# Four kilobytes of unused space behind each eight rows of an input in DRAM

## The chip, the core and the metric

The kernel runs on one core of a Trainium2 chip. The metric is the device time of one execution in microseconds (us). A core has engines that run side by side: TensorE (PE, with its weight loads shown apart as PEld), VectorE (DVE), ScalarE (ACT), GpSimd (POOL), and SyncE (SP), which here only issues DMAs. Sixteen DMA engines move data between DRAM and the on-chip memory SBUF, which has 128 partitions. Matmuls write to PSUM; DVE or ACT copy it from there to SBUF, which is called an eviction here.

## The reference

`x` is a 2048 x 1024 matrix in bf16. Two spectral filters A and B act on the same `x`, and a gate, one number for each row, mixes their results:

```python
g = sigmoid((x * gate_w).sum(-1, keepdims=True))
X = rfft2(x);  a = irfft2(X * (A_w_r + 1j*A_w_i));  b = irfft2(X * (B_w_r + 1j*B_w_i))
return g * a + (1 - g) * b
```

The inputs `A_x`, of which the kernel reads only one copy, and the four weight arrays of 2048 x 513 are read from DRAM, and a 2048 x 1024 result in bf16 is written.

## The kernel before

The Fourier transforms are written as small matmuls with constant matrices. The host sorts the rows of `x` so that a pair of row tiles (`j` and `j+1`) makes one block of 128 partitions by 2 by 1024 elements: `x_in` has the shape (8, 128, 2, 1024), so a partition's row of a block is 4096 bytes and a block is 512 KB without gaps. The columns are sorted so that sums and differences fold them.

L208 loads the eight blocks into the tiles `XR[0]` to `XR[7]` (`xr` in the profile). Blocks 0 and 7 are loaded in two halves of 256 KB, the others in one DMA, so there are ten DMAs, all issued by SP and all ahead of the constants and weights (L238 to L255), which SP issues in the same order behind them. SP waits before an issue until an earlier DMA has landed whose counter it reuses, eight DMAs back. ACT issues three small loads at the start, `f1` (L198), `gws` (L200, 16 bytes for each partition) and `sg` (L202, 4 bytes for each partition).

An order written out by hand (ORDER, a string of steps) sets what each engine does. Its first lines are the forward transform along the rows: `Vj` (function `xfold`, L295 and L296) forms a sum and a difference of `x[j]` on DVE, `rj` and `fj` (function `f1`, L312 and L321) are the matmuls with `x[j]`, or with what `xfold` made of it, as weights, and their evictions to `y` (L278 on ACT, L280 on DVE). For tiles 10 to 15 the steps `E` and `O` do the same for two tiles at once (L324). Then, for each of eight units `n` and both parities of the column frequency, `F` (f2, L375) transforms along the columns, `G` (f3, L394) goes on along the rows, `c` (L415) multiplies with the weights on DVE, and `i` (L453) begins the inverse. `F0` reads a part of `y` from every tile, so it waits for all of `x`.

The inverse stores its rows to scratch in DRAM (L461, `sc<-rl`) and fetches them back in another order (L470, `xr<-sc` and `ro<-sc`). A fetch reads 64 rows of 4096 bytes, each 32 KB behind the one before it. After that come `j` (L483, with the gate), `k` and `D` (L498 to L532), and the sums that make the output (L551 to L582).

Of the kernel before, what the change touches and what calls it, by code (L numbers as in the profile page):

```python
# [12 lines left out]
D = 1024  # L13
# [144 lines left out]
def gated_mix(ctx, tc, x_in, we_in, wo_in, gw_in, out):  # L158
    nc = tc.nc
# [44 lines left out]
    XR = [big.tile([P, 2064], BF16, name=f"xr{v}") for v in range(8)]  # L204
    RO = [big.tile([P, 2064], BF16, name=f"ro{v}") for v in range(8)]
    x = [XR[j // 2][:, 1024 * (j % 2):1024 * (j % 2) + 1024] for j in range(16)]
    for j0, n in ((0, 1), (1, 1)) + tuple((j, 2) for j in range(2, 14, 2)) + ((14, 1), (15, 1)):
        nc.sync.dma_start(XR[j0 // 2][:, 1024 * (j0 % 2):1024 * (j0 % 2 + n)].rearrange("p (j d) -> p j d", j=n), x_in[j0 // 2, :, j0 % 2:j0 % 2 + n, :])  # L208
    FD = const.tile([P, 2, 2, 2, 256], BF16, name="fd")
    IG = const.tile([P, 2, 4, 256], BF16, name="ig")  # L210
    WF = const.tile([P, NT, 3, 64], BF16, name="wf")
# [446 lines left out]
```

## Time and profile before

| | us |
|---|---|
| median of 3 runs | 114.53 |
| lowest and highest run | 112.67, 117.09 |
| the profiled execution | 113.11 |
| its span, first to last instruction | 111.3 |

The granted TensorE clock was 1.0 of full speed in the span. The DMA queues moved 37.07 MB in 18594 packets. The profile gives the busy time of each engine, groups of instructions by line of the code, who waited for whom, and when each DMA was issued and landed; times inside it count from the start of the span. "x<-y" is a tile written from a tile read, with buffer numbers left out. A few lines of the page on DMA, with the number of issues, the size of each and the median time from issue to landing:

```
xr<-sc SPq DMA_DIRECT2D x16, 256.0 KB, 5.2
ro<-in_we_dram SPq DMA_DIRECT2D x7, 516.0 KB, 8.4
xr<-in_x_dram SPq DMA_DIRECT2D x6, 512.0 KB, 8.4
xr<-in_x_dram SPq DMA_DIRECT2D x4, 256.0 KB, 5.7
```

### The profile page before, as it was taken

The numbers are of one execution on the slowest core, as the hardware profiler recorded it, in microseconds if no ns is written. First come the engines' busy times: TensorE is split into PE (matmuls) and PEld (weight loads), VectorE is DVE, ScalarE is ACT, GpSimd is POOL, SyncE is SP. The second block draws the span as 40 slices with busy tenths as digits, with TensorE's granted clock in tenths as the row PEclk, the third lists the DMA queues.
The fourth block names the chain that finished last, engine by engine and source line by source line (L and its number), as shares of the span: only waits on it lengthen the run. The fifth ranks groups of instructions, "written<-read, shape, count | busy, mean of one in ns | idle before, by whom it ended". The sixth has DMA issues, their size and how long they took to land. (4 is left out here: it accounts for less than half of the span.)

```text
span 111.3 us, 4030 instructions
## 1 busy us (share of the span) xinstructions
PE 99.1 (89%) x1656; PEld 68.5 (62%) x1656; DVE 92.3 (83%) x145; ACT 94.0 (84%) x185; POOL 7.4 (7%) x14
## 2 busy tenths in 40 slices
PE   5959989799999999999999999995999775999740
PEld 2339979475556658656765677654699564664430
DVE  0169957399899999999999999995989869699770
ACT  2246977599899999999999999999799798999740
POOL 1000000121592000000000000000000000000000
PEclk9999999999999999999999999999999999999999
DMA  3899999999999998995999999999995789998974
GB/s 106 223 361 415 405 397 406 414 411 388 412 397 409 398 333 262 367 392 181 260 359 334 363 316 386 362 317 378 322 276 217 224 228 358 399 408 358 366 281 128
DMA packets 18594, 37.07 MB, mean 333 GB/s; under 512 B 2188, under 2 KB 11024, under 8 KB 18576
## 3 DMA queue, kind: packets, MB, share of 16 engines
q1 hardware_dynamic: 17696, 36.37, 90.5%
q10 hardware_dynamic: 848, 0.45, 1.4%
q8 instruction: 13, 0.21, 0.7%
q14 instruction: 5, 0.04, 0.1%
q0 software_dynamic: 32, 0.00, 0.0%
HBM read 24.23 MB, written 12.58 MB: 331 GB/s over the span
## 5 line engine op out<-in xcount | busy, mean ns | idle before, releaser
L453 PE MATMUL pt<-p,wi 64*64 64x512 bf16 x488 | 30.6, 377 | 0.0
L278 ACT CAST rl<-pt 128x512 bf16<-128x512 f32 x47 | 28.6, 920 | 0.7 <-PE pt L453 0.7
L415 DVE TENSOR_TENSOR p<-X,ro 128x4096 bf16<-128x4096 bf16 x11 | 25.1, 2293 | 0.4 <-ACT V L344 0.3
L278 ACT CAST T<-pt 128x512 bf16<-128x512 f32 (+1 forms) x40 | 23.2, 721 | 1.6 <-PE pt L532 0.6
L453 PEld LDWEIGHTS <-wi 64*64 64x64 bf16 x488 | 16.1, 106 | 9.6 <-issue 1.5
L278 ACT CAST X<-pt 128x512 bf16<-128x512 f32 x27 | 17.5, 824 | 0.9 <-PE pt L394 0.9
L278 ACT CAST V<-pt 128x512 bf16<-128x512 f32 x28 | 16.3, 690 | 1.6 <-PE pt L483 1.5
L278 ACT CAST y<-pt 128x512 bf16<-128x512 f32 x21 | 11.2, 627 | 5.6 <-PE pt L321 4.1
L375 PE MATMUL pt<-fd,y 128*128 128x256 bf16 x128 | 15.9, 273 | 0.0
L375 PEld LDWEIGHTS <-y 128*128 128x128 bf16 x128 | 11.6, 98 | 4.3 <-issue 2.9
L280 DVE CAST rl<-pt 128x512 bf16<-128x512 f32 x17 | 11.2, 677 | 0.1
L394 PE MATMUL pt<-T,wf 64*64 64x512 bf16 (+2 forms) x192 | 10.5, 307 | 0.6 <-issue 0.6
L498 PE MATMUL pt<-ig,V 128*128 128x256 bf16 x88 | 10.8, 273 | 0.0
L574 DVE TENSOR_TENSOR rl<-wo,T 128x1024 bf16<-128x1024 bf16 (+1 forms) x18 | 9.2, 569 | 1.6 <-ACT T L278 1.2
L498 PEld LDWEIGHTS <-V 128*128 128x128 bf16 x88 | 8.2, 98 | 1.5 <-issue 0.4
L415 DVE TENSOR_TENSOR p<-X,wo 128x4096 bf16<-128x4096 bf16 x4 | 9.1, 2274 | 0.0
L280 DVE CAST y<-pt 128x512 bf16<-128x512 f32 x11 | 7.4, 686 | 2.1 <-PE pt L324 2.0
L278 ACT CAST p<-pt 128x512 bf16<-128x512 f32 x15 | 8.5, 604 | 0.3 <-PE pt L498 0.2
L394 PEld LDWEIGHTS <-wf 64*64 64x64 bf16 x192 | 5.6, 107 | 3.3 <-issue 1.2
L369 POOL TENSOR_SCALAR ro<-ro 128x8 bf16<-128x8 bf16 x7 | 5.8, 850 | 22.6 <-DMA ro<-in_we_dram 22.6
L483 PE MATMUL pt<-eab,ro 128*128 128x64 bf16 x128 | 5.0, 193 | 2.6 <-DMA ro<-sc 1.9
L483 PEld LDWEIGHTS <-ro 128*128 128x128 bf16 x128 | 4.5, 98 | 3.8 <-issue 2.5
(57 smaller groups left out, 107.7 us busy)
## 6 DMA issues: line engine op xcount, KB each, us to landing
sc<-rl SPq DMA_DIRECT2D x16, 512.0 KB, 6.0
xr<-sc SPq DMA_DIRECT2D x16, 256.0 KB, 5.2
ro<-sc SPq DMA_DIRECT2D x16, 256.0 KB, 5.5
ro<-in_we_dram SPq DMA_DIRECT2D x7, 516.0 KB, 8.4
xr<-in_x_dram SPq DMA_DIRECT2D x6, 512.0 KB, 8.4
out_dram<-rl SPq DMA_DIRECT2D x5, 512.0 KB, 4.3
wo<-in_wo_dram SPq DMA_DIRECT2D x4, 512.0 KB, 7.8
ro<-in_wo_dram SPq DMA_DIRECT2D x4, 512.0 KB, 6.7
```

The costliest lines, as they stand in the source:

```text
L278: nc.scalar.copy(out=out, in_=in_)
L280: nc.vector.tensor_copy(out=out, in_=in_)
L369: nc.gpsimd.tensor_scalar(Ws[n][:, :, :, 257:258], Ws[n][:, :, :, 256:257], -1.0, None, ALU.mult)
L375: nc.tensor.matmul(ps[tt][:, e * 256:e * 256 + 256], lhsT=y[par][:, c, e, t].rearrange("p b s k -> p (b s k)"), rhs=FD[:, par, c, e, :], s ...
L394: nc.tensor.matmul(ps[tt][ho, dst:dst + ln], lhsT=WF[hp(j), 2 * u + tt, w, :], rhs=T[hp(j), tt, src:src + ln], start=(k == 0), stop=(k == 2))
L415: nc.vector.tensor_tensor(po, xo, wo, ALU.mult)
L453: nc.tensor.matmul(ps[tt][hp(j), :], lhsT=WI[hin, 2 * u + tt, w, :], rhs=p[hin, q, tt, a::2, o:o + 256], start=(k == 0), stop=(k == len(te ...
L483: nc.tensor.matmul(ps[s][:, ch * 128 + h * 64:ch * 128 + h * 64 + 64], lhsT=R[:, k, ch * 128:ch * 128 + 128], rhs=EAB[:, 4 * v + k, :], st ...
L498: nc.tensor.matmul(po, lhsT=V[:, s, 2 * r + c, :], rhs=IG[:, par, 2 * r + c, :], start=(c == 0), stop=(c == 1))
L574: nc.vector.tensor_tensor(o4[:, k, h] if not isinstance(od, list) else o4[:, k.start, h], x, y_, op)
```

## The change

The host lays out each block of `x` as 16 groups of 8 rows and puts 2 x 1024 elements, 4096 bytes, of unused space behind each group. `x_in` becomes (8, 16, 18432): a group takes 36 KB in place of 32 KB and a block 576 KB in place of 512 KB. The unused bytes are not read. The load names the DRAM side as 16 groups by 8 rows by 1024 or 2048 elements, in place of 128 rows; the SBUF side is the same tile. Number, size and order of the DMAs stay, and so do all other instructions and their waits.

```diff
-        nc.sync.dma_start(XR[j0 // 2][:, 1024 * (j0 % 2):1024 * (j0 % 2 + n)].rearrange("p (j d) -> p j d", j=n), x_in[j0 // 2, :, j0 % 2:j0 % 2 + n, :])
+        nc.sync.dma_start(XR[j0 // 2][:, 1024 * (j0 % 2):1024 * (j0 % 2 + n)], x_in[j0 // 2, :, 0:8 * 2 * D].rearrange("a (b c) -> a b c", b=8)[:, :, 1024 * (j0 % 2):1024 * (j0 % 2 + n)])
...
     x = x.transpose(1, 0, 2, 3).reshape(P, 8, 2, D)
-    x = _np.ascontiguousarray(x.transpose(1, 0, 2, 3))
+    x = x.transpose(1, 0, 2, 3).reshape(8, 16, 8 * 2 * D)
+    x = _np.pad(x, ((0, 0), (0, 0), (0, 2 * D)))
```

## The prediction

> **What bounds the kernel now.** I read the page first: its busy shares, then its 40 slices, because the change touches only what is read in the first 16 us.
>
> ```profile
> PE 99.1 (89%) x1656; PEld 68.5 (62%) x1656; DVE 92.3 (83%) x145; ACT 94.0 (84%) x185; POOL 7.4 (7%) x14
> ...
> DMA  3899999999999998995999999999995789998974
> GB/s 106 223 361 415 405 397 406 414 411 388 412 397 409 398 333 262 367 392 181 260 359 334 363 316 386 362 317 378 322 276 217 224 228 358 399 408 358 366 281 128
> ```
>
> Three compute engines are busy over 80% of the span, in nearly every slice from the fourth on; whatever arrives late in the first slices moves all of that. Second, the table by stretches of the start, and for comparison the stretch of the last fetches (columns: us, busy time of PE, PEld, DVE, ACT, POOL, granted clock, DMA share, GB/s).
>
> ```profile
> 2.00:3.20 1.20, 1.20 (x4) 0.45 (x3) 0.00 (x0) 1.07 (x1) 0.00 (x0) 1.00 0.97 334
> 3.20:4.70 1.50, 1.50 (x4) 0.31 (x3) 0.00 (x0) 0.41 (x2) 0.00 (x0) 1.00 0.79 179
> 4.70:6.00 1.30, 1.30 (x15) 0.96 (x16) 0.70 (x8) 0.00 (x0) 0.00 (x0) 1.00 0.85 265
> 6.00:8.20 2.20, 1.11 (x22) 0.48 (x18) 1.35 (x5) 1.19 (x2) 0.00 (x0) 1.00 0.98 369
> 8.20:13.30 5.10, 5.07 (x121) 4.70 (x122) 5.09 (x12) 3.99 (x9) 0.00 (x0) 1.00 1.03 415
> ...
> 88.00:90.00 2.00, 0.81 (x22) 0.72 (x23) 2.00 (x5) 1.28 (x3) 0.00 (x0) 1.00 0.88 236
> 90.00:92.00 2.00, 2.00 (x32) 1.77 (x28) 0.98 (x3) 1.79 (x5) 0.00 (x0) 1.00 0.82 254
> 92.00:98.00 6.00, 4.79 (x78) 3.44 (x77) 4.77 (x10) 5.47 (x12) 0.00 (x0) 1.00 1.00 384
> ```
>
> Two things are to be seen. From 8.2 us the DMA engines move 415 GB/s, the highest of any stretch here. From 3.2 to 6.0 us they are 79% to 85% busy but move only 179 to 265: they hold packets that do not advance. The fetches show the same at 88 to 92 us. Third, the timeline of VectorE, which works on each pair's block (xfold) as it lands.
>
> ```profile
> 8.21 0.42 DVE L295 TENSOR_TENSOR rl<-xr 128x512 bf16<-128x512 bf16 x1 [0.86 <-DMA xr<-in_x_dram]
> 8.55 0.42 DVE L296 TENSOR_TENSOR rl<-xr 128x512 bf16<-128x512 bf16 x1
> 8.89 0.69 DVE L280 CAST y<-pt 128x512 bf16<-128x512 f32 x1
> 9.49 0.42 DVE L295 TENSOR_TENSOR rl<-xr 128x512 bf16<-128x512 bf16 x1
> 9.83 0.42 DVE L296 TENSOR_TENSOR rl<-xr 128x512 bf16<-128x512 bf16 x1
> 10.16 0.69 DVE L280 CAST y<-pt 128x512 bf16<-128x512 f32 x1
> 10.77 0.43 DVE L295 TENSOR_TENSOR rl<-xr 128x512 bf16<-128x512 bf16 x1
> ```
>
> It starts on a block at 8.21, 9.49, 10.77 and 12.11. The landings in the trace, DMA by DMA, are 3.61 and 5.02 (the two halves of block 0), then 8.19, 9.46, 10.75, 12.02, 13.30, 14.58 (blocks 1 to 6), 15.24 and 15.92. Each start follows its landing by 0.02 to 0.09 us. So x has **no slack**: what x loses, the start loses, and from 13.5 to 18.7 us PE is busy 5.0 of 5.4 us with the rest of that step, so nothing there gives it back. The weights behind x do have slack: the first lands at 18.4 and is multiplied at 22.98.
>
> **The change part by part.** No compute instruction changes and no wait changes; ten DMAs of L208 keep sizes and order. Three things differ.
>
> (1) Pitch in DRAM. Rows of a block stay 4096 B apart within groups of eight; groups go from 32 KB to 36 KB apart. The bytes moved stay, 4.19 MB, in packets of 2048 and 4096 B. In stream a 512 KB block takes 1.28 us (410 GB/s), and 4096 B packets have a median of 159 ns. The fetches (L470) read rows that lie 32 KB apart; once they stream they land each 0.63 us for 256 KB, 416 GB/s. So a 32 KB pitch costs nothing in stream, and the pad gains 0 there. [...]
>
> What the pad could gain is the stall at 3.2 to 6.0 us. At the streaming pace block 1 would land at 3.61+0.67+1.28=5.6 instead of 8.19: 2.6 us are lost. But the kernel cannot take all of that. Weight loads need 0.77+0.54=1.31 us a block and DVE 0.34+0.34+0.60=1.28, so from its first block on the start is as slow as the DMA. With block 1 early, VectorE gains its wait of 0.86 us and PE 0.92. Only if gws (landing 5.20, first engine 3.97) came earlier too would V1 move from 6.00 to about 4.8, 1.2 more. Bound of the gain: 0.9 to 2.0 us.
>
> (2) Form of the DMA. Before, both sides are 128 rows. After, the DRAM side is 16 groups of 8 rows and the SBUF side 128 rows of 1. In the built program the x loads lose a mark that every 128-row load carries and the 64-row fetches do not. Rows for this: SP's issue takes 328 to 333 ns for a marked load with nothing ahead, 451 to 468 for a fetch. That is 0.13 us for each issue. Two count, those of block 0, since the DMA queue is filled ahead from then on: +0.1 to 0.3 us; I take 0.2.
>
> (3) Which engine takes which rows. No view shows it for either form. With 16 groups on the DRAM side an even split over 16 engines is one group each, which lands in eight neighbouring partitions. The nearest row is the fetch: 64 rows, unmarked, four an engine. Its stream is at full rate, but its start is poor: the fetches from 85.4 us on land at 88.42, 89.78, 92.03, 92.66, 93.27 and 93.91, where 0.63 apart the last would be at 91.6. So 2.3 us go until the engines have drawn apart, and packets of 0.3 to 1.8 us stand in that stretch. Bounds: 0 (the present stall of 2.6 us is the same thing and is only replaced) and, if engines stayed in each other's way throughout, half of the 410 GB/s: 10.2 us of stream again, +9 as an upper end (10.2 less what lands before 4.7). I take one such start-up loss on top of the present one, 2.5, nearest to the only row of such a form.
>
> [...]
>
> **Sum**: 113.11 us (span 111.3 and 1.8 around it) +0.2 +2.5 = 115.8. The median shown, 114.53, lies 1.4 above that execution, and its runs lie 112.67 to 117.09; on its scale 117.2, of which I give 117.0. From 2% on (2.3 us) a measurement of this kernel tells a difference from none.
>
> **The rivals.**
>
> *Slower by a new start-up loss (forecast)*, 117.0, its own range 116 to 121. For it: the unmarked fetches lose 2.3 us at each start, and x has no slack. Against: their rows all lie 32 KB apart, which the padded groups no longer do. Chance 0.45: of it 0.1 beyond 119, where the engines do not draw apart.
>
> *Nothing but the issue cost.* The stall at 3.2 to 6.0 is the first small loads (gws, 16 B rows, and sg, 4 B rows) that run between x's packets there, and the pad does not touch them; the split does no harm. +0.2 to +0.5: 114.8. For it: gws lands at 5.20 and sg at 8.38, just in the stall, and the first 2048 B loads, with the same pitch, ran at 334 GB/s from 2.0 to 3.2. This covers too that the change does not do what it says, for instance that rows are served in another order than addresses suggest. Chance 0.35.
>
> *Faster: the stall goes.* Engines that start together read 16 or 32 KB apart and meet in the same part of DRAM; with 36 KB they do not. It decides if packets at 3.4 to 4.7 us, now 0.4 to 1.35 us, fall to 159 ns. Price: 0.9 to 2.0 us, so 112.5 to 113.6 on the median's scale; over 2% only if the other runs, up to 117.09, lose more in that stall than the profiled one. For it: output stores, which only write DRAM, do not stall when they start, fetches do. [...] Chance 0.2, with most of it near 2%.
>
> **How the numbers follow.** Slower by over 2%: 0.45 less 0.03 that stays within, 0.42. Faster by over 2%: 0.2 less 0.04, plus 0.02 for medians that scatter, 0.18. Within: 0.40. The range leaves out the half rate beyond 121.5 and the lowest tail: 112.0 to 121.5.
>
> **What the profile after would show.** The landings of blocks 1 and 6: 8.19 and 14.58 now, about 2.7 later by the forecast, 0.2 later by the second, 1 to 2.6 earlier by the third. VectorE's wait on xr at L295, 0.86 us once: longer or repeated, the same, or gone. GB/s from 8.2 to 13.3 us: below 415 means collisions that last. SP's issue at L208 should go from 328 to about 450 ns. F0's first matmul, at 18.71, moves with x. I am wrong if blocks land 1.28 us apart from 8.2 us or sooner, and wrong about the place if x lands as now and the time is gained or lost after 20 us.

## The result and the profile after

| | before | after |
|---|---|---|
| median of 4 runs, us | 113.6 | 116.91 |
| lowest and highest run | 112.56, 117.09 | 116.19, 117.04 |
| the profiled execution | 113.11 | 116.85 |
| its span | 111.3 | 115.1 |

The kernel became slower, by a ratio of 1.037 (95% interval 1.030 to 1.044). The profiled executions differ by 3.74 us. Executions of one kernel can differ by some per cent (17 of the kernel before, beside the last experiments, gave 111.0 to 118.06 us): ratios here and below leave the slow ones out, no ratio is given where only one or two others are left, and profiles are read for the first part alone.

The page of the kernel after, its first lines and the DMA lines of its 40 slices:

```profile
PE 99.6 (87%) x1656; PEld 68.0 (59%) x1656; DVE 92.7 (81%) x145; ACT 94.2 (82%) x185; POOL 8.7 (8%) x14
...
DMA  2999999999999999998999999989959889998973
GB/s 77 246 273 265 269 256 277 407 410 416 390 407 382 421 400 395 357 392 302 283 313 357 312 309 375 371 257 347 383 203 278 288 221 357 386 409 349 359 294 97
```

The engines have the same work (PE 99.6 us against 99.1), so the time is idle time. The two DMA lines belong together: from the second slice on the DMA engines are busy over 90%, yet until the seventh they move 246 to 277 GB/s, where the same slices of before reached 415. The table by stretches of the start says it more exactly (columns as in the prediction: us, busy time of PE, PEld, DVE, ACT, POOL, granted clock, DMA share, GB/s):

```profile
2.00:3.20 1.20, 1.20 (x4) 0.46 (x3) 0.00 (x0) 1.01 (x1) 0.00 (x0) 1.00 0.73 220
3.20:4.70 1.50, 1.25 (x4) 0.30 (x2) 0.00 (x0) 0.47 (x2) 0.00 (x0) 1.00 0.94 221
4.70:6.00 1.30, 1.05 (x16) 0.70 (x16) 1.02 (x8) 0.14 (x1) 0.00 (x0) 1.00 0.90 287
6.00:8.20 2.20, 0.80 (x17) 0.46 (x18) 1.11 (x4) 1.06 (x2) 0.00 (x0) 1.00 0.99 277
8.20:13.30 5.10, 4.13 (x90) 3.50 (x92) 3.87 (x9) 3.21 (x7) 0.00 (x0) 1.00 1.03 264
13.30:18.70 5.40, 4.19 (x124) 3.58 (x119) 3.44 (x7) 3.48 (x7) 0.00 (x0) 1.00 1.03 263
18.70:23.00 4.30, 3.80 (x101) 3.39 (x95) 2.45 (x4) 2.67 (x6) 0.27 (x1) 1.00 1.05 365
```

At 8.2 to 13.3 us stands 264 where 415 stood, at the same DMA share of 1.03, and it is no better at 13.3 to 18.7. VectorE follows the blocks of x; its timeline in the kernel after, the lines of L295:

```profile
8.17 0.42 DVE L295 TENSOR_TENSOR rl<-xr 128x512 bf16<-128x512 bf16 x1 [1.09 <-DMA xr<-in_x_dram]
...
10.17 0.42 DVE L295 TENSOR_TENSOR rl<-xr 128x512 bf16<-128x512 bf16 x1 [0.63 <-DMA xr<-in_x_dram]
...
12.13 0.43 DVE L295 TENSOR_TENSOR rl<-xr 128x512 bf16<-128x512 bf16 x1 [0.60 <-DMA xr<-in_x_dram]
...
14.16 0.42 DVE L295 TENSOR_TENSOR rl<-xr 128x512 bf16<-128x512 bf16 x1 [0.67 <-DMA xr<-in_x_dram]
```

The first start is where it was (8.21 before). The next ones come 2 us apart in place of 1.28, and VectorE now waits at each of these four blocks, where before it waited once, 0.86 us. The landings of the last packet of each DMA in the two traces:

| block of x | 0 (halves) | 1 | 2 | 3 | 4 | 5 | 6 | 7 (halves) |
|---|---|---|---|---|---|---|---|---|
| before | 3.61, 5.02 | 8.19 | 9.46 | 10.75 | 12.02 | 13.30 | 14.58 | 15.24, 15.92 |
| after | 4.70, 5.70 | 8.15 | 10.15 | 12.11 | 14.07 | 16.05 | 17.90 | 18.90, 20.09 |

So block 1 lands where it did, and then each block loses 0.67 us on average: blocks 1 and 6 land 9.75 us apart in place of 6.40 (+3.35), block 7 takes 2.19 in place of 1.33 (+0.85), and x ends 4.17 later. That block 1 is not late does not show that the form is free up to there. Block 0 is 0.7 to 1.1 us late, the GB/s stand at 220 to 287 from 2.0 us on, and the small load `sg` lands at 5.91 in place of 8.38; three other kernels below with this form land block 1 at 7.82, 8.89 and 9.61. The packets agree with the pace: 4096 B took a median of 159 ns before and 253 ns after (8 to 16 us). The 128 of a block, shared evenly by sixteen engines (an estimate), are eight for each: 1.27 and 2.02 us, close to the 1.28 and 1.97 between blocks.

How the loss travels, from the timelines of both: F0's first matmul 18.71 to 21.85 (+3.14), multiply c4 35.55 to 38.56 (+3.01), multiply c8 49.90 to 53.45 (+3.55), the end 111.34 to 115.07 (+3.73). Some 1.0 us of x's 4.17 is won back before F0: between the last landing and F0 lie 1.76 us where 2.79 lay, since the engines, now kept waiting for x, have less queued up behind it. Some 0.5 us is added between c4 and c8. Of that, 0.3 us is a wait of PE at L357 for an eviction of VectorE, which before had none there; the rest was not followed.

SP's issue of the x loads, the source line L208 in the kernel before and after (ns: least, median, most):

```profile
L208 SPq DMA_DIRECT2D xr<-in_x_dram x10: 328/423/792, 0.7 to 8.4; - x10
```

```profile
L208 SPq DMA_DIRECT2D xr<-in_x_dram x10: 578/603/737, 0.7 to 6.8; - x10
```

The least goes up by 0.25 us.

### The profile page after: what moved, and what is told of

Read it like the earlier page. It is cut to its first block, busy times and chain, and to the rows that moved or that the text cites. A ratio compares the mean times of both kernels' runs of the same rounds, so it can differ in the third digit from the quotient of the medians.

```text
span 115.1 us, 4030 instructions
## 1 busy us (share of the span) xinstructions
PE 99.6 (87%) x1656; PEld 68.0 (59%) x1656; DVE 92.7 (81%) x145; ACT 94.2 (82%) x185; POOL 8.7 (8%) x14
## 5 line engine op out<-in xcount | busy, mean ns | idle before, releaser
L278 ACT CAST rl<-pt 128x512 bf16<-128x512 f32 x47 | 28.1, 923 | 1.2 <-PE pt L453 0.7
L369 POOL TENSOR_SCALAR ro<-ro 128x8 bf16<-128x8 bf16 x7 | 6.7, 979 | 25.7 <-DMA ro<-in_we_dram 25.6
L321 PE MATMUL pt<-f,xr 64*128 64x256 bf16 x80 | 5.2, 270 | 2.9 <-DMA xr<-in_x_dram 2.9
L324 PE MATMUL pt<-f,xr 64*128 64x128 bf16 x192 | 6.1, 216 | 1.2 <-DMA xr<-in_x_dram 1.0
```

Source lines behind the costliest of these rows:

```text
L278: nc.scalar.copy(out=out, in_=in_)
L321: nc.tensor.matmul(pv[h][:, :, c, :, :].rearrange("p a e k -> p e a k"), lhsT=xs(j0, h, q), rhs=fs(h, 0, *st), start=(q == 0), stop=(q == 3))
L324: nc.tensor.matmul(pv[h][:, a, c, :, :], lhsT=xs(items[a][0], h, q), rhs=fs(h, items[a][1] * st[1], st[0]), start=(q == 0), stop=(q == 3))
L369: nc.gpsimd.tensor_scalar(Ws[n][:, :, :, 257:258], Ws[n][:, :, :, 256:257], -1.0, None, ALU.mult)
```

## The experiments

Two questions were open. Is it the **form** of the load (16 groups of 8 rows, and perhaps with it another split of the rows over the DMA engines) or the **pitch** in DRAM (36 KB in place of 32 KB)? And if the form, is it the side in DRAM or the side in SBUF that costs? Every kernel below starts from the kernel before and changes only the loads of x (and the host's layout for it) unless said; the compute stays whole. Of the longer edits only the main lines are shown.

### The form without the large gap

The load of the kernel after, with 256 bytes behind each 8 rows in place of 4096. (With no gap at all the 16 x 8 rows lie at one pitch, as the 128 rows of before do, so the gap can't be zero.)

```diff
-    x = _np.pad(x, ((0, 0), (0, 0), (0, 2 * D)))
+    x = _np.pad(x, ((0, 0), (0, 0), (0, 128)))
```

> The load of the changed kernel (16 groups of 8 rows on the DRAM side), but with 256 bytes of unused space behind each group in place of 4096: the pitch of a group is 32.25 KB. The changed kernel's blocks of x land 1.97 us apart, the kernel before's 1.28. Theory A, the split: the form hands each DMA engine eight neighbouring partitions and engines get in each other's way on the SBUF side, whatever lies in DRAM; blocks land 1.97 us apart, at 264 GB/s, and the time is 1.03 to 1.045 of before. Rival B, the pitch: 36 KB between the rows that engines read at one time is the bad distance in DRAM; with 32.25 KB the blocks land 1.28 us apart and the time is 1.00 to 1.01.

120.32 us (median of 4; the kernel before beside it 113.56), ratio 1.066 (1.056 to 1.077). Blocks land 2.15 us apart; 4096 B packets have a median of 276 ns (8 to 14 us). Its table by stretches:

```profile
8.20:13.30 5.10, 3.65 (x46) 2.90 (x48) 2.73 (x6) 1.60 (x3) 0.00 (x0) 0.67 1.04 244
```

The loss is there without the 36 KB pitch, and larger than Theory A had it (1.97 us, 264 GB/s, 1.03 to 1.045). The pitch does not cause it.

### The pitch without the form

128 plain rows, each with 512 unused bytes behind it: rows lie 4608 bytes apart, 8 rows 36 KB, as in the kernel after.

```diff
+        nc.sync.dma_start(XR[j0 // 2][:, 1024 * (j0 % 2):1024 * (j0 % 2 + n)], x_in[j0 // 2, :, 1024 * (j0 % 2):1024 * (j0 % 2 + n)])
...
+    x = x.transpose(1, 0, 2, 3).reshape(8, P, 2 * D)
+    x = _np.pad(x, ((0, 0), (0, 0), (0, 256)))
```

> The load of the kernel before (128 rows on both sides), but with 512 bytes of unused space behind each row: rows lie 4608 bytes apart, so eight rows take 36 KB as in the changed kernel. Theory A, the split: the form is that of before, so blocks land 1.28 us apart and the time is 0.99 to 1.01 of before. Rival B, the pitch of 36 KB for eight rows: blocks land about 1.97 us apart, time 1.03 to 1.045. A third reading, C, that rows 4096 bytes apart cause the stall at 3.2 to 6.0 us of before: block 1 lands up to 2.6 us earlier than 8.2 us, and the time is 0.98 to 0.99.

111.31 to 113.74 us in 4 runs. Blocks land 1.28 us apart, block 1 at 7.76. It was run again, to see whether the 0.4 us by which block 1 came earlier is a gain:

> Rows 4608 bytes apart once more, with more rounds. In its first run block 1 landed at 7.76 us in place of 8.2 and the blocks 1.28 us apart. If the 0.4 us earlier come from the pitch, the ratio is 0.990 to 0.997; if they are chance, 0.997 to 1.005. A ratio of 1.03 would bring the pitch of 36 KB for eight rows back as the cause.

Ratio 1.005 (0.995 to 1.015), block 1 at 8.17. Its table by stretches in that second run:

```profile
8.20:13.30 5.10, 5.09 (x122) 4.72 (x124) 5.10 (x12) 4.00 (x9) 0.00 (x0) 1.00 1.03 415
```

415 GB/s, as before the change. A pitch of 36 KB for 8 rows neither costs nor gains beyond that interval, and the 7.76 did not come again. So the form is what costs.

### DRAM or SBUF: four ways to load half a block

Blocks 1 to 6 are each loaded by two DMAs of 64 rows, 256 KB. The rows are consecutive in DRAM or 8 KB apart; their places are 64 neighbouring partitions or every second one. All four combinations were run. The first two take the layout as it is:

```diff
+            for h in range(2):
+                nc.sync.dma_start(XR[j0 // 2][64 * h:64 * h + 64, 0:2048], x_in[j0 // 2, 64 * h:64 * h + 64].rearrange("p j d -> p (j d)"))
```

> Rows in DRAM as before, without unused space; each of the blocks 1 to 6 is loaded in two DMAs, one for partitions 0 to 63 and one for 64 to 127, of 64 rows each on both sides. An even split over 16 engines gives an engine four neighbouring partitions. Theory A, that engines meet on the SBUF side when the partitions in work at one time are few or neighbours: a half takes longer than the 0.64 us of the stream, 1.0 to 1.3 us, so a block 2.0 to 2.6 us; time 117 to 120 us. Rival D, that only the grouped form on the DRAM side is slow and not where the data goes: a block each 1.28 us, time 113 to 114.5 us.

```diff
+            for h in range(2):
+                nc.sync.dma_start(XR[j0 // 2][h::2, 0:2048], x_in[j0 // 2, h::2].rearrange("p j d -> p (j d)"))
```

> Rows in DRAM as before; each of the blocks 1 to 6 is loaded in two DMAs of 64 rows, one for the even partitions and one for the odd, so each covers all 128 partitions' range as the fetches (L470) do. The fetches land 0.63 us apart once they stream. Theory A: the halves stream at the fetches' pace, a block each 1.28 us, perhaps with up to 2.3 us lost at the start; time 113 to 116 us. Rival E, that any load of 64 rows is slower when it reads x: a block each 1.9 us or more, time 117 us.

In the other two the host reorders the rows, so that the two sides change places: consecutive rows to every second partition, and rows 8 KB apart to neighbouring partitions.

```diff
+                nc.sync.dma_start(XR[j0 // 2][h::2, 0:2048], x_in[j0 // 2, 64 * h:64 * h + 64].rearrange("p j d -> p (j d)"))
...
+    x[1:7] = x[1:7].reshape(6, 64, 2, 2, D).transpose(0, 2, 1, 3, 4).reshape(6, P, 2, D)
```

> Blocks 1 to 6 in two DMAs of 64 rows each. The rows of a DMA lie one behind the other in DRAM, as in the run with neighbouring halves (1.10 us for 256 KB), but go to every second partition, as in the run with every second row (0.61 to 1.15 us, mean 0.76). The host has put the rows in that order. Theory A, the place in SBUF decides: 256 KB each 0.63 to 0.8 us, time 113 to 116. Rival F, the rows in DRAM decide (64 rows in 256 KB without gaps are read by too few parts of DRAM at a time): 1.10 us, time about 117.

```diff
+                nc.sync.dma_start(XR[j0 // 2][64 * h:64 * h + 64, 0:2048], x_in[j0 // 2, h::2].rearrange("p j d -> p (j d)"))
...
+    x[1:7] = x[1:7].reshape(6, 2, 64, 2, D).transpose(0, 2, 1, 3, 4).reshape(6, P, 2, D)
```

> The cross to the one before: the rows of a DMA lie 8 KB apart in DRAM and go to 64 neighbouring partitions. Theory A, the place in SBUF decides: 256 KB each 1.10 us, time about 117. Rival F, the rows in DRAM decide: 0.63 to 0.8 us, time 113 to 116.

| | to 64 neighbouring partitions | to every second partition |
|---|---|---|
| consecutive rows in DRAM | 1.09 to 1.16 us a half, packets 285 ns | 0.58 to 0.71 us between stalls, packets 159 ns |
| rows 8 KB apart in DRAM | 1.08 to 1.12 us, packets 286 ns | 0.61 to 1.15 us, mean 0.79, packets 159 ns |

(Packet times are medians of those of 4096 B. The loads to every second partition stall at times: one half of consecutive rows took 2.14 us, one 0.86. Into neighbours the two halves of block 6 took longer than the others, 1.16 to 1.69.) The stretches of the four, in the order e3, f2 (neighbours), f1, e4 (every second); of f1 the stretch ahead of its long stall, while over 8.2 to 13.3 us it moves 371 GB/s:

```profile
8.20:13.30 5.10, 3.66 (x89) 3.12 (x84) 3.40 (x8) 3.35 (x7) 0.00 (x0) 1.00 1.04 236
```

```profile
8.20:13.30 5.10, 3.65 (x85) 2.96 (x80) 3.31 (x7) 3.62 (x7) 0.00 (x0) 1.00 1.03 237
```

```profile
8.20:11.20 3.00, 3.00 (x76) 2.88 (x72) 2.84 (x8) 3.00 (x7) 0.00 (x0) 1.00 0.99 388
```

```profile
8.20:13.30 5.10, 5.07 (x134) 4.79 (x130) 5.00 (x12) 5.05 (x11) 0.00 (x0) 1.00 0.99 350
```

236 and 237 into neighbours, 350 and 388 into every second partition, whatever the rows in DRAM. **For these loads of 64 rows the place in SBUF decides.** F0 says the same: it starts at 22.11 and 21.92 us with neighbours (e3, f2), and at 18.30 and 17.16 with every second partition (f1, e4), where 18.71 stood before the change. The times, of one run each (117.18, 115.63, 113.75, 115.49 in the order of the diffs), decide nothing, since the kernel before alone gave 111.12 to 116.63 beside the last two; in e4 the mean granted clock was 0.97 besides, where e3 had 1.00. One step is open: a load into 64 neighbours covers half of the partitions, while the kernel after fills all 128 in one DMA, so the four loads show that the place can cost as much, not that it costs there in the same way.

### The grouped form into every second partition

16 groups of 4 rows with 4096 bytes behind each, to every second partition: the grouped form, taken out of neighbouring partitions.

```diff
+                xg = x_in[j0 // 2].rearrange("(g c) -> g c", g=32)[16 * h:16 * h + 16, 0:4 * 2 * D]
+                nc.sync.dma_start(XR[j0 // 2][h::2, 0:2048], xg.rearrange("a (b c) -> a b c", b=4))
```

> Blocks 1 to 6 in the grouped form with 4096 bytes of unused space, but 16 groups of 4 rows to a DMA, which go to every second partition. Theory A: what the group form costs is the neighbouring partitions that it hands out, so with every second partition 256 KB take 0.63 to 0.8 us, time 113 to 116. Rival D, the grouped form itself is slow: 1.0 us or more, time 116.5 to 118.

```profile
8.20:13.30 5.10, 3.95 (x91) 3.39 (x87) 3.52 (x8) 4.09 (x8) 0.00 (x0) 1.00 1.04 308
```

0.89 us a half, packets with a median of 220 ns (8.2 to 13.3 us), 308 GB/s, one run of 115.31 us: between the expectations, and a miss for both. In this trace the rate is above that of the kernel after (264) and below that of the same rows ungrouped (388, or 371 with the stall). A theory of place alone does not give this number. It is one execution, though, and the grouped form shows other paces too, up to 378 GB/s (under "A larger gap"), so how much of the 308 is the grouping is not shown.

### Three of the blocks

The load of the kernel after for blocks 1 to 3 alone, to see whether a block's loss stands for itself.

```diff
+        if j0 in (2, 4, 6):
+            xg = x_in[j0 // 2].rearrange("(g c) -> g c", g=16)[:, 0:8 * 2 * D]
+            nc.sync.dma_start(XR[j0 // 2][:, 0:2048], xg.rearrange("a (b c) -> a b c", b=8))
+            continue
```

> The changed kernel's load (groups of 8 rows, 4096 bytes behind each) for blocks 1 to 3 only; blocks 0 and 4 to 7 as in the kernel before. If each grouped block costs 1.97-1.28=0.69 us and x has no slack, block 6 and the end come 2.1 us later: ratio 1.015 to 1.022. If the loss comes from the first DMAs alone (block 0 in its two halves) or from what follows x, the ratio is 1.00 to 1.005.

Blocks 1 to 3 land at 8.89, 11.08 and 13.31, 2.2 apart, and the others 1.28 apart from 14.44 on: the loss stops with the form. x ends at 18.35 (+2.4), F0 starts at 20.79 (+2.1). The time is 1.041 (1.021 to 1.060) of before; the expected size fits only the lower end of that. Two stretches of this kernel, a grouped and a plain one:

```profile
8.30:11.10 2.80, 2.05 (x32) 1.64 (x32) 1.36 (x3) 0.94 (x2) 0.00 (x0) 0.75 1.04 257
14.40:18.40 4.00, 4.00 (x130) 3.75 (x126) 3.45 (x7) 3.72 (x8) 0.00 (x0) 1.00 1.04 392
```

The expectation had taken 1.97 us a block, and 2.2 is what this run shows for the same form and gap. The ratio stands for more than the 2.1 us seen at F0; where the rest is lost was not followed.

### A larger gap

8192 bytes behind each 8 rows.

```diff
-    x = _np.pad(x, ((0, 0), (0, 0), (0, 2 * D)))
+    x = _np.pad(x, ((0, 0), (0, 0), (0, 4 * D)))
```

> The changed kernel with 8192 bytes behind each 8 rows in place of 4096. Blocks of x landed 2.15 us apart with 256 bytes, 1.97 with 4096, and 2.2 where only blocks 1 to 3 had the form with 4096. Theory A, that engines meet in SBUF and how much depends on how far they happen to be apart in time: somewhere from 1.9 to 2.3 us, in no order with the size of the space; time 116 to 121. Rival G, that the unused space relieves the grouped form in DRAM, more space more: 1.8 us or less, time 114.5 to 116.

```profile
8.20:13.30 5.10, 5.10 (x122) 4.46 (x118) 4.86 (x12) 4.25 (x9) 0.00 (x0) 1.00 1.04 378
13.30:18.70 5.40, 4.44 (x150) 4.03 (x146) 2.83 (x6) 3.65 (x8) 0.00 (x0) 1.00 1.04 297
```

Blocks 2 to 5 land 1.38 to 1.45 us apart at 378 GB/s, the sixth 2.01 behind the fifth; one run, 117.37 us. Theory A's 1.9 to 2.3 is missed: the form does not always run at one pace. The 1.40 us fit rival G, by which more space relieves the form, but its time of 114.5 to 116 does not, and the rate falls to 297 right after. What may go with the pace is seen in the sixteen landings that the trace has of each DMA (without saying whose). In the kernel after (blocks 2 to 5) and in g1 (blocks 3 to 5) their offsets stay the same from block to block within some 0.06 us; in f4 they shift by up to 0.6 us, though the blocks end 2.2 us apart each time. The spread from first to last differs from kernel to kernel:

| kernel | gap, bytes | us between blocks | spread of a block's 16 landings, us |
|---|---|---|---|
| e1 | 256 | 2.15 | 3.1 to 3.4 |
| f4, blocks 1 to 3 | 4096 | 2.2 | 2.8 to 3.2 |
| after | 4096 | 1.97 | 1.9 |
| g1, blocks 3 to 5 | 8192 | 1.40 | 1.4 |

One gap, 4096, has given 1.97 and 2.2, so the gap alone does not set the pace; how far apart a block's landings lie when the stream begins may. It would have to be a matter of the grouped form: plain rows kept 1.27 to 1.28 us with a spread of 2.1 to 2.6 (before) and of 1.1 to 1.3 (the kernel c2 below). No run forced the spread, and whether it or the gap sets the pace stays open.

### The stall ahead of block 1

The prediction's second and third rival blamed the stall at 3.2 to 6.0 us on the small loads (`gws`, `sg`) or on the pitch. Here both loads go behind x, to SP's queue after the first weights, and the seven VectorE instructions that read `gws` go into `gate_hat`, ahead of its matmuls.

```diff
-    nc.scalar.dma_start(gws[:], gw_in)
...
-    nc.scalar.dma_start(sg[:], dr["SG"])
...
     load_w(0)
+    nc.sync.dma_start(gws[:], gw_in)
+    nc.sync.dma_start(sg[:], dr["SG"])
```

> The kernel before with two small loads (gws, 16 bytes a partition, and sg, 4 bytes a partition) moved from ACT's queue at the start to SP's behind the first weight load, and VectorE's seven small operations on gws moved to just before the gate's matmuls. Theory H, these loads make the stall at 3.2 to 6.0 us: block 1 lands at 5.6 to 6.5 us in place of 8.2, VectorE starts on it at once, and the time is 0.982 to 0.992 of before. Rival I, the stall is that of engines which start together: block 1 lands at 8 us as before, ratio 0.995 to 1.005.

and the same with the 4608-byte rows:

> The run before with x's rows 4608 bytes apart as well (128 rows on both sides). If the small loads are the stall and the row pitch does nothing, the same as the run before. If the pitch matters too (engines that start together meet in the same part of DRAM), block 1 lands 0.3 to 1 us earlier than there, and the time is 0.975 to 0.985 of before.

Block 1 lands at 7.23 in the first and at 6.47 in the second, against 8.19. The first is later than the 5.6 to 6.5 that was expected; its GB/s are 367 and 290 in the stretches shown here for the second:

```profile
3.20:4.70 1.50, 1.50 (x4) 0.31 (x4) 0.33 (x1) 0.00 (x0) 0.00 (x0) 1.00 1.05 407
4.70:6.00 1.30, 1.30 (x17) 0.97 (x18) 0.43 (x2) 0.00 (x0) 0.00 (x0) 1.00 1.03 378
```

179 and 265 GB/s stood there before. In the second the stall is gone and F0 starts at 17.19 in place of 18.71 (17.96 in the first). The 0.76 us between the two block 1s fits the expectation that the row pitch matters too, but each is one execution, and 4608-byte rows alone gave 7.76 and 8.17. Neither kernel is faster, against both expectations: 112.97 to 118.15 us for the first, and the second 1.036 (1.025 to 1.047) of before. A reason is in the first kernel's timelines of PE and VectorE:

```profile
28.78 1.91 PE L339 MATMUL pt<-y,gwz 128*32 128x512 bf16 x32 [2.88 <-DVE gwz L332]
```

```profile
25.86 2.30 DVE L413 TENSOR_TENSOR p<-X,ro 128x4096 bf16<-128x4096 bf16 x1
28.07 0.17 DVE L326 TENSOR_SCALAR gh<-gws 128x8 f32<-128x8 bf16 x1
```

The moved instructions stand on VectorE behind a multiply of 2.30 us, and PE waits 2.88 us for them, which is more than the start had won. The second kernel shows the same wait, at 26.92 us. So c4 comes at 37.68 and 37.14 in place of 35.55; how the second comes to 1.036 from there was not followed. The move took away all or part of the stall and put its own wait later; a version that does only the first was not run.

## Why the prediction was right or wrong

The direction was right, and 117.0 us stands beside a median of 116.91. That closeness is luck: the sum gave +2.7 us and the profiled executions show +3.74, by another mechanism than the one it named, while the median of before that it was added to, 114.53, became 113.6 with a fourth run. The two errors, each about 1 us, cancel.

**Part 1, the pitch: right.** "The pad gains 0 there" holds: 36 KB for 8 rows gave 1.005 (0.995 to 1.015) and 415 GB/s.

**Part 2, the issue: the term was mis-sized, and it can't be seen by itself.** The least issue went up by 0.25 us (328 to 578 ns), not 0.13. Block 0's halves land 0.7 to 1.1 later, but block 1 at 8.15 against 8.19, so no +0.2 was left by then.

**Part 3, which engine takes which rows: the failed step.** The term "one such start-up loss, 2.5" says that the engines lose once and then draw apart. No such single loss is seen, block 1 landing at 8.15 as before, and while x streamed they never came to full rate: +3.35 us over blocks 1 to 6 and +0.85 on block 7, at 264 GB/s with no recovery by 18.7 us. That is the forecast's own tail, "where the engines do not draw apart", which had 0.1 and was placed beyond 119, since half rate, an estimate of the author's, was its only price. No run streamed x at half of 410 GB/s (the least, in e3 over 13.3 to 18.7 us, is 231), and the measured pace, 64% of full rate, is milder. The row it took, the fetch, was a wrong neighbour: L470 writes `[g::2]`, every second partition, and this is the place at which the ungrouped loads f1 and e4 ran at 350 to 388 GB/s. Read together with its SBUF side, that row gives no price for eight neighbouring partitions an engine. What the runs show in place of the start-up loss is a lower rate for as long as the form lasts (f4: 257 GB/s with it, 392 after it), with the form as its cause and not the pitch (e1, e2b). Why the form is slow is argued: loads into 64 neighbours are slow however the rows lie in DRAM (236 and 237 GB/s), but that the grouped form gives each engine eight neighbouring partitions no view shows, and f3 and g1 show that place alone does not set the pace.

Packets of 4096 B had medians of 253 ns (after) and 276 to 280 ns (e1, f4) in place of 159; which engine writes where the traces do not show.

**"x has no slack": right up to x's end, 1.0 us too strict behind it.** "Nothing there gives it back" was argued from a busy PE at 13.5 to 18.7 us. But that was work that had piled up, and with slower blocks it is done earlier: x ended 4.17 us later, F0 started 3.14 later.

**The rivals.** "Nothing but the issue cost" fell with its time, 114.8. Its account of the stall stands in part: with the two small loads out of the way block 1 came 1.0 us earlier (c1), and 1.7 with the longer rows as well (c2), of the 2.6 us that the prediction counted as lost. "Faster: the stall goes" fell with its time, and its cause with e2b, where 4608-byte rows alone left 161 GB/s at 4.7 to 6.0 us. The kernel after can't tell whether a stall is left: its 221 to 287 GB/s from 3.2 to 8.2 us lie around the 264 at which it goes on.

**The signs named beforehand.** Block 6 was to land about 2.7 us later, and block 1 too: block 6 landed 3.32 later, block 1 did not. A repeated wait on xr and under 415 GB/s at 8.2 to 13.3 us, by the prediction "collisions that last", came as named, and the latter sign was the one that told a start-up loss from a lasting one.

## What to carry to other kernels

A gap that breaks the even pitch of the rows turns a load of 128 rows into a load of groups, and here that cost 36% of the DMA rate while the gap itself gained nothing; if rows must be padded, pad every row alike, which was free here. When a price is taken from another DMA of the trace, compare both its sides: these loads of 64 rows ran at 236 and 237 or at 350 to 388 GB/s by their partitions alone. A DMA share of 1.03 with the GB/s down by a third meant here that each packet took longer (253 ns in place of 159), not that work was lacking, and the first stretches in steady stream tell whether that is a start-up loss or a new pace.

## What the runs showed that was not expected

The sixteen landings of a DMA can keep their offsets. In the kernel after, the first and the last landing of blocks 2 to 5 lie 1.90 to 1.92 us apart every time, and the sixteen repeat within some 0.06 us. It is not always so: in the kernel before the spread goes from 2.56 to 2.09 over blocks 1 to 4 at one pace, and in g1 from 1.38 to 1.97 from block 5 to block 6, where the pace breaks.

The granted TensorE clock fell after a long wait for x. In the kernel with the 256-byte gap PE idles 2.81 us ahead of block 1; its timeline and its stretches:

```profile
9.65 1.89 PE L321 MATMUL pt<-f,xr 64*128 64x256 bf16 x16 [2.81 <-DMA xr<-in_x_dram]
...
13.94 1.05 PE L321 MATMUL pt<-f,xr 64*128 64x256 bf16 x16
```

```profile
9.60:11.30 1.70, 1.65 (x16) 1.18 (x18) 1.36 (x3) 0.00 (x0) 0.00 (x0) 0.50 1.03 243
11.30:13.30 2.00, 2.00 (x34) 1.72 (x30) 1.36 (x3) 1.60 (x3) 0.00 (x0) 0.60 1.06 250
13.30:15.00 1.70, 1.70 (x46) 1.50 (x42) 1.08 (x3) 1.39 (x3) 0.00 (x0) 1.00 1.02 239
```

The same sixteen matmuls take 1.89 us at a clock of 0.50 and 1.05 us at 1.00. The kernel after, with 1.15 us as PE's longest wait there, kept 1.00 in every stretch shown. In f4 VectorE waits 1.68 us for block 1 (1.09 in the kernel after), and the clock is 0.75 at 8.3 to 11.1 us, 0.67 over 8.2 to 13.3 and 1.00 from there to 18.7. The length of the wait does not settle it: the same wait of 2.88 us of PE for VectorE stands ahead of gate matmuls, 32 in each kernel, that take 1.91 us in c1 (shown above) and 3.23 in c2; the mean granted clocks of the two spans are 0.996 and 0.965:

```profile
26.92 3.23 PE L339 MATMUL pt<-y,gwz 128*32 128x512 bf16 x32 [2.88 <-DVE gwz L332]
```

So a wait may cost more than its length. In e1 and f4 that did not show at F0, which came 5.44 and 2.08 us later while x ended 6.47 and 2.43 later.
